# Seven half products for the second matmul in two of every three token groups in place of every second one, and for 17 tokens as well as 16

## The chip, the core and the metric

The kernel runs on one core of a Trainium2 chip. The metric is the device time of one execution in microseconds; unless said otherwise, a number is the median of the fast runs of a kernel. Ratios are the mean time of one kernel's fast runs over that of the kernel before in the same rounds, so not quite the ratio of the medians that stand beside them. Where a length comes from a trace, it is one profiled execution.

In the profiles here TensorE (PE) does the matmuls, VectorE (DVE) elementwise work, transposes and statistics, ScalarE (ACT) activations and copies, GpSimd (POOL) next to nothing (11.1 us, 1% of the span).

## The reference

```python
# x (8, 4224, 192) fp32; weight (8 heads, 7 taps)
out = causal_conv_7_taps(x, softmax(weight))      # one tap set per head of 24 channels
mu, var = mean(out), var(out)                     # over the 192 channels
xn = (out - mu) / sqrt(var + 1e-6) * g_ln
return out + relu(xn @ w_ch1) @ w_ch2             # 192 -> 768 -> 192
```

## The kernel before

Each of 128 partitions holds 33 tokens of each of 8 batches, which the kernel works through in 18 groups: 6, 8, 9 and 10 tokens, then 16 (even groups) and 17 (odd groups) by turns. For group `g` TensorE runs `up(g)` (first matmul, `ph` in the profile; ScalarE applies the ReLU) and then the second matmul, in one of two ways: in full (`down`, `po`) or in seven half products after Strassen and Winograd (`down_fast`, `pd`). Meanwhile VectorE prepares the next group: six of the seven taps (`conv`; the first is ScalarE's), then a transpose (`yt`) which `up(g + 1)` reads. That transpose is called the hand-over below. A group with the seven products is "fast", the others "slow"; F16 is a fast group of 16 tokens, S17 a slow one of 17.

```python
for g in range(NG):
    if g + 2 < NG: load_x(g + 2)
    up(g)
    ...
    if g in FAST:                       # fast group: all of this is VectorE's but down_fast
        conv(g + 1, 1, 4)               # three taps of the next group
        sums_early(g, (0,))             # sums of halves of the hidden layer
        conv(g + 1, 4, 5)
        sums_early(g, (1, 2))
        parts = down_fast(g)            # TensorE: seven products; VectorE: conv(g+1,5,6),
                                        #   sums_late (six ops), the first of three adds
        conv(g + 1, 6, 7)
        transpose(g + 1)                # the hand-over
        stats(g)
        finish_fast(g, *parts)          # two adds, six transposes, residual, store
        continue
    if g + 1 < NG:                      # slow group
        conv(g + 1); transpose(g + 1)
    ...
    stats(g); down(g); finish(g)
```

In `down_fast` the third product reads what `sums_early` wrote, the fifth and the seventh what `sums_late` wrote. VectorE runs its instructions in this order, as its timelines show (in group 9 after the change the taps at 509.72 us start only after the sums that waited for the ReLU until 507.19), and the buffers of the hidden layer, of the transposed input and of the products' results are single.

Of the kernel before, what the change touches and what calls it, by code (L numbers as in the profile page):

```python
# [16 lines left out]
def kernel(  # L17
# [54 lines left out]
    assert max(n for _, _, n in groups) <= J  # L72
    NG = len(groups)

    FAST = set(range(6, NG - 1, 2))
    NFAST = max(groups[g][2] for g in FAST)
    T = C // 2
    CH = NC // 2
# [223 lines left out]
    def conv(g, k0=1, k1=K):  # L302
        n = groups[g][2]
        t = xg[g]
        for k in range(k0, k1):
            for h in range(H):
                cs = slice(h * GRP, h * GRP + GRP)
                nc.vector.scalar_tensor_tensor(  # L308
                    out=y[g][:, 0:n, cs], in0=t[:, k : k + n, cs], scalar=taps[:, h, k : k + 1],
                    in1=y[g][:, 0:n, cs], op0=ALU.mult, op1=ALU.add,  # L310
                )
# [59 lines left out]
    def up(g):  # L371
        n = groups[g][2]
        t = yt[g]
        room = hpool.tile([P, NF * NQ * J * C], F32, tag="ht", name=f"ht{g}")
        if g in FAST:

# [5 lines left out]
        for f in range(NF):  # L382
            fs = slice(f * P, f * P + P)
            for js in blocks(n):
# [12 lines left out]
                for q in range(NQ):  # L397
                    src = ph[q][:, 0:w]
                    if g in FAST:
                        dst = ht[g][:, :, f // FC, f % FC, q, js, :].rearrange("p h j t -> p j h t")  # L400
# [33 lines left out]
    def w2_sums():  # L434
        (b11, b12), (b21, b22) = (
            (w2[:, e * FC : e * FC + FC, 0 : D // 2], w2[:, e * FC : e * FC + FC, D // 2 : D])
            for e in range(2)
        )

        for dst, a, b in ((0, b12, b11), (1, b22, 0), (2, b22, b12), (3, b21, 1)):  # L440
            a, b = (w2sums[:, v] if isinstance(v, int) else v for v in (a, b))
            nc.vector.tensor_tensor(w2sums[:, dst], a, b, op=ALU.subtract)
# [147 lines left out]
    for g in range(NG):  # L590
# [3 lines left out]
        if g == 4:  # L594
            w2_sums()
        if g in FAST:
            conv(g + 1, 1, 4)
# [57 lines left out]
```

## Time and profile before

1045.72 us (1045.59 to 1046.34, 4 runs), granted TensorE clock 1.00. From the chain of waits and VectorE's timeline that the prediction shows:

| part | F16 | S17 | S16 |
|---|---|---|---|
| group, us of TensorE | 58.44 | 66.35 | 62.15 |
| the hand-over is ready, us before TensorE needs it | 2.6 | some 22 | some 25 |

The first row is the sum of two pieces of the chain. The last row is the end of the `yt` transpose against the start of the next group, for S17 and S16 worked out from the timeline.

### The profile page before, as it was taken

The numbers are of one execution on the slowest core, as the hardware profiler recorded it, in microseconds if no ns is written. First come the engines' busy times: TensorE is split into PE (matmuls) and PEld (weight loads), VectorE is DVE, ScalarE is ACT, GpSimd is POOL, SyncE is SP. The second block draws the span as 40 slices with busy tenths as digits, with TensorE's granted clock in tenths as the row PEclk, the third lists the DMA queues.
The fourth block names the chain that finished last, engine by engine and source line by source line (L and its number), as shares of the span: only waits on it lengthen the run. The fifth ranks groups of instructions, "written<-read, shape, count | busy, mean of one in ns | idle before, by whom it ended". The sixth has DMA issues, their size and how long they took to land.

```text
span 1044.5 us, 35348 instructions
## 1 busy us (share of the span) xinstructions
PE 1025.0 (98%) x16088; PEld 661.1 (63%) x16088; DVE 877.0 (84%) x1981; ACT 347.0 (33%) x890; POOL 11.1 (1%) x23
## 2 busy tenths in 40 slices
PE   4999999999999999999999999999999999999998
PEld 2988554358545775458654686556854578545876
DVE  7999999949479996799967999679977899679913
ACT  4442332315034340344304442144412445033320
POOL 1000000000000000000000000000000000000000
PEclk9999999999999999999999999999999999999999
DMA  5113113012030030302112030300303003010101
GB/s 190 60 63 137 47 78 122 1 62 89 3 148 2 13 138 3 148 2 95 57 58 92 3 150 2 140 10 3 150 2 149 1 3 150 2 65 2 54 11 67
DMA packets 7315, 67.15 MB, mean 64 GB/s; under 512 B 1151, under 2 KB 1919, under 8 KB 3326
## 3 DMA queue, kind: packets, MB, share of 16 engines
q1 hardware_dynamic: 6862, 64.91, 16.3%
q8 instruction: 125, 2.05, 0.8%
q14 instruction: 24, 0.20, 0.1%
q10 hardware_dynamic: 304, 0.00, 0.0%
HBM read 38.95 MB, written 25.95 MB: 62 GB/s over the span
## 4 chain that ended last, share of the span: by engine, by line
PE 91%; DVE 7%; DMA 1%; ACT 0%; issue 0%; DVEq 0%; SPq 0%
PE ph L393 47%; PE po L425 29%; PE pd L487 16%; DVE y L308 4%; DMA room<-in_moe_w_ch_dram 1%; DVE yt L320 0%; DVE st L333 0%; DVE y L568 0%; DVE ot L561 0%; ACT room L186 0%; DVE room L194 0%; DVE spare L194 0%; DVE w L200 0%; ACT spare L186 0%; DVE d L355 0%
## 5 line engine op out<-in xcount | busy, mean ns | idle before, releaser
L393 PE MATMUL ph<-yt,w 32*128 32x256 f32 (+4 forms) x7200 | 517.8, 443 | 0.5 <-DVE ot L561 0.5
L393 PEld LDWEIGHTS ph<-yt,w 32*128 32x128 f32 x7200 | 367.9, 185 | 147.9 <-issue 115.5
L308 DVE SCALAR_TENSOR_TENSOR y<-xg,taps,y 128x384 f32<-128x384 f32 (+5 forms) x864 | 431.4, 576 | 0.0
L405 ACT ACTIVATE ht<-ph 128x288 f32<-128x288 f32 (+4 forms) x600 | 222.7, 458 | 545.3 <-PE ph L393 545.2
L425 PE MATMUL po<-ht,w 128*32 128x256 f32 (+6 forms) x5760 | 328.9, 390 | 0.0
L425 PEld LDWEIGHTS po<-ht,w 128*32 128x32 f32 x5760 | 184.6, 110 | 142.7 <-issue 24.8
L561 DVE STREAM_TRANSPOSE ot<-po 128x288 f32<-128x288 f32 (+6 forms) x114 | 47.3, 448 | 105.2 <-PE po L425 105.0
L487 PE MATMUL pd<-ht,w 128*32 128x256 f32 x1296 | 72.3, 379 | 0.0
L487 PE MATMUL pd<-ht,w2sums 128*32 128x256 f32 x1296 | 71.0, 379 | 0.0
L333 DVE BATCH_NORM_STATS2 st<-y 128x6 f32<-128x192 f32 x264 | 69.7, 342 | 0.0
L298 ACT ACTIVATE y<-xg,taps 128x384 f32<-128x384 f32 (+4 forms) x136 | 69.5, 602 | 0.0
L487 PEld LDWEIGHTS pd<-ht,w 128*32 128x32 f32 x1296 | 41.5, 110 | 31.3 <-issue 4.5
L487 PEld LDWEIGHTS pd<-ht,w2sums 128*32 128x32 f32 x1296 | 42.1, 110 | 27.8
L320 DVE STREAM_TRANSPOSE yt<-y 128x3072 f32<-128x3072 f32 (+5 forms) x18 | 56.0, 3112 | 3.0 <-PE ph L393 1.8
L568 DVE SCALAR_TENSOR_TENSOR y<-ot,r,y 128x192 f32<-128x192 f32 x168 | 57.1, 412 | 0.7
L454 DVE TENSOR_TENSOR s<-ht 128x1024 f32<-128x1024 f32 x18 | 22.0, 1222 | 38.7 <-ACT ht L405 38.7
L492 ACT COPY cs<-pd 128x256 f32<-128x256 f32 x72 | 27.0, 375 | 48.8 <-PE pd L487 48.8
L492 ACT COPY part<-pd 128x256 f32<-128x256 f32 x54 | 20.1, 372 | 40.6 <-PE pd L487 40.6
L536 DVE SCALAR_TENSOR_TENSOR y<-ot,r,y 128x192 f32<-128x192 f32 x96 | 32.1, 411 | 0.2
L487 PE MATMUL pd<-s,w2sums 128*32 128x256 f32 x432 | 24.4, 379 | 0.0
L455 DVE TENSOR_TENSOR ht<-ht 128x1024 f32<-128x1024 f32 x18 | 22.1, 1225 | 0.6
L531 DVE STREAM_TRANSPOSE ot<-cs 128x512 f32<-128x512 f32 x36 | 22.0, 674 | 0.0
(70 smaller groups left out, 199.7 us busy)
## 6 DMA issues: line engine op xcount, KB each, us to landing
xg<-in_x_dram SPq DMA_DIRECT2D x7, 2208.0 KB, 12.1
xg<-in_x_dram SPq DMA_DIRECT2D x7, 2112.0 KB, 11.6
out_dram<-y SPq DMA_DIRECT2D x7, 1536.0 KB, 6.0
out_dram<-y SPq DMA_DIRECT2D x6, 1632.0 KB, 6.2
xg<-in_x_dram SPq DMA_DIRECT2D x1, 1536.0 KB, 6.3
xg<-in_x_dram SPq DMA_DIRECT2D x1, 1440.0 KB, 6.0
xg<-in_x_dram SPq DMA_DIRECT2D x1, 1344.0 KB, 10.8
raw<-in_moe_w_ch_dram SPq DMA_DIRECT2D x1, 1152.0 KB, 8.1
```

What stands on the lines that cost most here:

```text
L298: nc.scalar.mul(dst, src, tap)
L308: nc.vector.scalar_tensor_tensor(out=y[g][:, 0:n, cs], in0=t[:, k : k + n, cs], scalar=taps[:, h, k : k + 1], in1=y[g][:, 0:n, cs], op0=AL ...
L320: nc.vector.transpose(yt[g][:, 0:n].rearrange("p j c t -> p (j c t)"), y[g][:, 0:n].rearrange("p j d -> p (j d)"),)
L333: nc.vector.bn_stats(out=st[:, j, :], in_=y[g][:, j, :])
L393: nc.tensor.matmul(ph[q][:, 0:w], w1[rows, c, fs], t[rows, js, c, :], start=(c == 0), stop=(c == NC - 1),)
L405: nc.scalar.activation(dst, src, AF.Relu)
L425: nc.tensor.matmul(bank[C * q : C * q + C, 0:w], w2[:, f, C * c : C * c + C], t[:, f, q, js, :], start=(f == 0), stop=(f == NF - 1),)
L487: nc.tensor.matmul(dst[C * q : C * q + C, 0:w], right[:, f, C * c : C * c + C], left[:, f, q], start=(first and f == 0), stop=(f == FC - 1 ...
L492: nc.scalar.copy(to[:, c], dst[:, 0:w].rearrange("p (j t) -> p j t", t=T))
L536: nc.vector.scalar_tensor_tensor(out=yg[:, j, :], in0=ot[:, j, :], scalar=rstd[g][:, j : j + 1], in1=yg[:, j, :], op0=ALU.mult, op1=ALU.add,)
L561: nc.vector.transpose(ot[:, js, C * c : C * c + C], src.rearrange("p (j t) -> p j t", t=C))
L568: nc.vector.scalar_tensor_tensor(out=yg[:, j, :], in0=ot[:, j, :], scalar=rstd[g][:, j : j + 1], in1=yg[:, j, :], op0=ALU.mult, op1=ALU.add,)
```

## The change

The seven products cost TensorE less than the full one, and the change uses them in eight groups instead of six; the groups of 17 tokens are new to them.

```diff
-    FAST = set(range(6, NG - 1, 2))
+    FAST = {g for g in range(6, NG - 1) if g % 3 != 2}
```

Before: 6, 8, 10, 12, 14, 16. After: 6, 7, 9, 10, 12, 13, 15, 16. For the first time two fast groups follow each other, in the order F16, F17 (6-7, 12-13) and in the order F17, F16 (9-10, 15-16). In the instruction order nothing else moves. The buffers of the products' results become 17 tokens wide, so the adds of a group of 16 have one dimension more; they still take 0.95 us.

## The prediction

One label in the text below is wrong: the worked example, which begins at 415.13 us, is group 8, not group 6 (group 6 begins at 290.33 and has the same lengths), and the slow group after it is 9. The steps use only its lengths.

The forecast's sum is 1045.76 - 9.1 + 1.4 = 1038.1; the lags behind its 1.4 us use the early and late sums of 17 tokens on VectorE, 7.6 and 7.2 us, which took an allowance for each instruction. The measured 7.2 and 6.8 us of 16 tokens times 17/16 give 7.65 and 7.2 (an estimate), so VectorE's 63.7 us and the lags stand on that. In the trace before, one such sum of 1024 elements took 1216 to 1225 ns on average. The 0.1 us for the signal to TensorE, part of the 1.4, was the author's estimate; the only number near it in the trace before is the 0.07 us from TensorE's end to VectorE's start in group 4.

> **What bounds the kernel now.** I read the page's engine shares first, then the chain of waits in order of time, then a table of windows by group, then VectorE's timeline inside one of the groups that use seven half products. Group 6 is the example; the kernel has 18 groups (0 to 17) of 6, 8, 9, 10 and then 16 and 17 tokens by turns, and "fast" below means a group that uses the seven products, "slow" one that doesn't. F16 is a fast group of 16 tokens, S17 a slow one of 17.
>
> ```profile
> span 1044.5 us, 35348 instructions
> ...
> PE 1025.0 (98%) x16088; PEld 661.1 (63%) x16088; DVE 877.0 (84%) x1981; ACT 347.0 (33%) x890; POOL 11.1 (1%) x23
> ...
> PEclk9999999999999999999999999999999999999999
> ```
>
> ```profile
> 381.99 33.14 PE po L425 x576
> 415.13 31.11 PE ph L393 x288
> 446.24 27.33 PE pd L487 x504
> 473.57 33.21 PE ph L393 x576
> 506.79 33.14 PE po L425 x576
> 539.92 31.11 PE ph L393 x288
> ```
>
> In the chain of waits (start, length, what) every piece from 87.07 us to 1039.54 us is TensorE, each beginning where the one before ended. So there TensorE never waits, and each group has a fixed price: F16 = 31.11 + 27.33 = 58.44 us, S17 = 33.21 + 33.14 = 66.35 us. Group 4, the only S16, has pieces of 31.11 (from 161.83) and 31.04 us (from 192.95) in the same view: 62.15 us. ph is the first matmul, po the second in full, pd the second in seven half products.
>
> ```profile
> core 0: us, PE busy (x) PEld busy (x) DVE busy (x) ACT busy (x) POOL busy (x), PEclk, DMA share, GB/s
> ...
> 415.13:473.57 58.44, 58.44 (x796) 30.95 (x796) 51.82 (x86) 23.42 (x52) 1.05 (x1) 1.00 0.18 68
> 473.57:539.92 66.35, 66.35 (x1157) 48.05 (x1156) 57.15 (x147) 19.72 (x57) 0.00 (x0) 1.00 0.16 60
> ```
>
> VectorE is busy 51.8 of 58.4 us and 57.2 of 66.4 us: it looks loose, but its work for group 6 is not done inside group 6's window, as its timeline shows (start, length, line, what, idle before it):
>
> ```profile
> 419.21 13.38 DVE L308 SCALAR_TENSOR_TENSOR y<-xg,taps,y 128x408 f32<-128x408 f32 x24
> 438.06 1.23 DVE L454 TENSOR_TENSOR s<-ht 128x1024 f32<-128x1024 f32 x1 [5.46 <-ACT ht L405]
> ...
> 440.46 4.51 DVE L308 SCALAR_TENSOR_TENSOR y<-xg,taps,y 128x408 f32<-128x408 f32 x8
> ...
> 455.19 3.48 DVE L465 TENSOR_TENSOR ht<-s,ht 128x1024 f32<-128x1024 f32 x3
> 458.60 3.48 DVE L467 TENSOR_TENSOR ht<-ht 128x1024 f32<-128x1024 f32 x3
> ...
> 467.42 3.58 DVE L320 STREAM_TRANSPOSE yt<-y 128x3264 f32<-128x3264 f32 x1
> 470.93 4.21 DVE L333 BATCH_NORM_STATS2 st<-y 128x6 f32<-128x192 f32 x16
> ...
> 488.91 25.48 DVE L308 SCALAR_TENSOR_TENSOR y<-xg,taps,y 128x384 f32<-128x384 f32 x48
> 514.50 3.38 DVE L320 STREAM_TRANSPOSE yt<-y 128x3072 f32<-128x3072 f32 x1
> ```
>
> Group 6 begins on TensorE at 415.13. VectorE joins it at +4.1 us (419.21), idles 5.5 us for the ReLU of the fourth block, hands over the transposed input of group 7 at 470.93 (+55.8; TensorE needs it at +58.44), and is done with group 6 at 488.91 (+73.8), which is 15.3 us into group 7. The slow group gives this lag back.
>
> [...]Here 144 products of 512 columns took 31.04 us, 215.6 ns each[...], 252 of 256 columns 27.33 us, 108.5 ns[...], and 288 of 288 and 256 columns by turns 33.14 us, 115.1 ns[...], and the granted clock is 1.00.[...]
>
> **The change part by part.** Fast groups were 6, 8, 10, 12, 14, 16 (all of 16 tokens). They become 6, 7, 9, 10, 12, 13, 15, 16: four of 16 and four of 17 tokens, so 132 tokens in place of 96. Slow are 8, 11, 14 and 17.
>
> TensorE. A conversion of 17 tokens replaces 33.14 us by 252 products of 272 columns. 272 is the mean of the 288 and 256 that now take 115.07 ns, so 252 x 115.07 = 29.0 us: 4.14 us saved. A conversion of 16 saves 31.04 - 27.33 = 3.71. Before 6 x 3.71 = 22.26; after 4 x 3.71 + 4 x 4.14 = 31.40. Gain 9.1 us, if TensorE still never waits.
>
> VectorE. Its work in a fast group, measured start to start in the timeline above, with next group of 17: six taps 26.7 us, early sums 7.2, late sums 6.8, one add 0.9, transpose 3.5, statistics 7.3, two adds 1.7, output transposes 3.7, residual 5.3: 63 us, against 58.4 of TensorE. F17 with next 16: taps 25.7, early sums 7.6[...], late sums 7.2, adds 2.8, transpose 3.3, statistics 7.6, output 3.9 + 5.6: 63.7 us, against 33.21 + 29.0 = 62.2. Slow groups need some 46 us against 62 to 66. Over a cycle of three (63 + 63.7 + 46 = 173 against 183 to 187 of TensorE) VectorE still fits. But two fast groups in a row are new: the lag of the first is now carried into a second which also wants more than it gives. So I followed it through, times from each group's start on TensorE.
>
> Order F16, F17 (6-7 and 12-13). The second starts with VectorE at +15.3. Three taps to 28.1; early sum 30.7, tap 34.9, two early sums 40.0 (their ReLUs are there by about 34.4); tap 44.3; late sums 51.5; add 52.4; tap 56.8; transpose 60.1. TensorE needs it at 62.2: 2.1 us to spare. TensorE's third product, which reads the early sums, starts at 33.2 + 2 x 4.14 = 41.5; the fifth, which reads the late ones, at 49.8 while the first late sums are ready at 47.9. Nothing waits. VectorE leaves at +79.0, 16.8 into the slow group.
>
> Slow group 8 (S16). Taps and transpose end at 47.0, statistics at 54.3, then VectorE is ahead of the products again: it waits for the last of six. In group 4 the last output transpose began 0.07 us after TensorE's end (224.05) and the residual ended at 230.08, so VectorE enters group 9 at +6.1.
>
> Order F17, F16 (9-10 and 15-16). F17 from +6.1: taps to 18.9, wait for the ReLU to about 23.5, transpose ends at 57.1 (needed 62.2), VectorE leaves at 76.0, i.e. +13.8. F16 from +13.8 with 17-wide taps: 27.2; early sum 29.6, tap 34.0, early sums 38.8 (the third product starts at 38.9); tap 43.3; late sums 46.7 and 50.1 (the fifth product starts at 46.7, and reads the last third of them 0.9 us later); add 51.0; tap 55.5; transpose 59.0, but TensorE needs it at 58.44. Here TensorE waits, 0.6 us plus some 0.1 for the signal. Twice: 1.4 us. Group 11 then starts with VectorE at +17.9; its ninth output bank (of eight) needs the first one transposed at 55.3, and VectorE gets there at 54.4. It just fits.
>
> ScalarE does 21 copies of 272 elements (some 0.39 us, estimated between the 0.375 of 256 and more) and eight first taps in the seven products, as in every fast group now; at 33% busy it is not asked for more than it has. The loads move later, because one load waits for the residual of two groups earlier: issued at +15 to +18, 12 us to landing, needed on ScalarE from about +34. Hidden.
>
> Sum: 1045.76 - 9.1 + 1.4 = 1038.1.
>
> **Rivals.** (1) VectorE becomes the bound. Busy share 84% and 63 us against 58.4 speak for it; the slow third group with 16 to 20 us of spare time speaks against it, as long as the lag is given back there. If each fast group cost 2 us more on VectorE than I reckon (strided 17-token tiles, an add with one more dimension), the order F17, F16 would wait some 4.5 us and F16, F17 some 2, each twice: 13 us, and the time would be 1045.76 - 9.1 + 13 = 1050. (2) No wait at all: my chain is conservative by 1 us a group, and the gain is 9.1: 1036.6. The before timeline fits my durations to 0.1 us, so a whole microsecond is unlikely. (3) A buffer holds: y with three buffers, or the x loads with two, now released by the second fast group's residual, arriving late for ScalarE's first tap. That would show as ScalarE waiting for a transfer[...]. The 4 us between landing (about +30) and need (+34) in the slow group, where ScalarE has nothing else to do, speak against it.
>
> **Range and chances.** Prediction 1038.1 us, 0.7% less. The floor is 1036.6, since nothing else is removed; above it the waits could be several times my 1.4 us. 8 times in 10 within 1036.4 to 1043. 2% is 21 us: the whole saving of TensorE is 9 us, so faster by over 2% is next to impossible, 0.01. Slower by over 2% would need 30 us of new waits, about 7 in each of four pairs, 0.02. Within 2%: 0.97.
>
> **What would show it.** The pd pieces of groups 7, 9, 13, 15 last 29.0 us and po pieces of S16 31.04. The idle time of TensorE or its weight load before ph, put down to VectorE's transpose, appears only at the starts of groups 11 and 17, under 1 us each. VectorE's first tap after group 7's residual starts some 16.8 us into group 8, that of group 11's some 17.9 us into it. VectorE's idle time before the early sums vanishes in groups 7, 10, 13, 16. I'd be wrong if pd or po waits for VectorE in the middle of a group, if waits also stand at the starts of groups 8 and 14, or if 272 columns cost more than 115 ns.

## The result, and the profile after

1038.12 us (1038.00 to 1038.75, 4 runs) against 1045.72: ratio 0.9927, 95% interval 0.9910 to 0.9945. The page after:

```profile
span 1036.2 us, 33980 instructions
...
PE 1015.6 (98%) x15368; PEld 644.4 (62%) x15368; DVE 910.0 (88%) x1987; ACT 363.9 (35%) x932; POOL 11.1 (1%) x23
...
PE 74%; DVE 22%; issue 2%; DMA 1%; ACT 1%; DVEq 0%; SPq 0%
```

TensorE lost 9.4 us of busy time and VectorE gained 33, and the chain that ended last, 91% TensorE before, now goes through VectorE for 22% of the span. That share does not mean that VectorE cost 22%: the chain is followed back from one wait to its releaser, and a short wait is enough to switch it to VectorE's long unbroken row of work. How long the waits are is told by TensorE's own timeline (start, length, what, and in brackets the idle time before it):

```profile
410.49 31.18 PE L393 MATMUL ph<-yt,w 32*128 32x512 f32 x288
...
472.64 33.28 PE L393 MATMUL ph<-yt,w 32*128 32x288 f32 x576
...
534.87 31.18 PE L393 MATMUL ph<-yt,w 32*128 32x512 f32 x288
...
589.32 4.07 PE L487 MATMUL pd<-ht,w 128*32 128x256 f32 x72
594.06 33.28 PE L393 MATMUL ph<-yt,w 32*128 32x288 f32 x576 [0.68 <-DVE yt L320]
...
964.65 33.28 PE L393 MATMUL ph<-yt,w 32*128 32x288 f32 x576 [0.68 <-DVE yt L320]
```

These are the starts of groups 8, 9, 10, 11 and 17. Only 11 and 17, the groups after F17, F16, have an idle time, and it is put down to the hand-over. The windows by group give the price of each (busy times and counts as in the prediction's table of windows):

```profile
core 0: us, PE busy (x) PEld busy (x) DVE busy (x) ACT busy (x) POOL busy (x), PEclk, DMA share, GB/s
...
348.27:410.49 62.22, 62.22 (x1084) 45.70 (x1080) 61.50 (x118) 27.25 (x77) 0.00 (x0) 1.00 0.17 64
534.87:594.06 59.19, 58.51 (x796) 30.86 (x793) 58.54 (x100) 24.20 (x54) 1.05 (x1) 1.00 0.17 67
```

Group 7 (F17) takes 62.22 us where it took 66.35 as S17. Group 10 takes 59.19 us where F16 without a wait takes 58.44. VectorE's lag shows in its own timeline:

```profile
427.24 26.69 DVE L308 SCALAR_TENSOR_TENSOR y<-xg,taps,y 128x408 f32<-128x408 f32 x48
...
478.80 12.79 DVE L308 SCALAR_TENSOR_TENSOR y<-xg,taps,y 128x384 f32<-128x384 f32 x24
...
548.67 13.39 DVE L308 SCALAR_TENSOR_TENSOR y<-xg,taps,y 128x408 f32<-128x408 f32 x24
561.98 1.23 DVE L454 TENSOR_TENSOR s<-ht 128x1024 f32<-128x1024 f32 x1
...
590.34 3.58 DVE L320 STREAM_TRANSPOSE yt<-y 128x3264 f32<-128x3264 f32 x1
593.84 4.22 DVE L333 BATCH_NORM_STATS2 st<-y 128x6 f32<-128x192 f32 x16
```

Subtract each group's start on TensorE: VectorE enters slow group 8 at 427.24 - 410.49 = +16.8 us, group 9 at 478.80 - 472.64 = +6.2 (the slow group gave 10.6 us back), group 10 at +13.8. There it no longer idles before the early sums, which had 5.5 us of idle time before them in the kernel before, and is through with the hand-over at +59.0, when TensorE would have started at +58.44.

What sets the +13.8 is not the lag at which VectorE enters group 9. There VectorE waits twice for the ReLU, 6.2 us in all:

```profile
496.19 1.29 DVE L454 TENSOR_TENSOR s<-ht 128x1088 f32<-128x1088 f32 x1 [4.59 <-ACT ht L405]
...
507.19 1.29 DVE L454 TENSOR_TENSOR s<-ht 128x1088 f32<-128x1088 f32 x1 [1.62 <-ACT ht L405]
```

After the second wait (+34.6 in group 9) it has no idle time up to the hand-over in group 10. So an earlier entry into group 9, or one up to some 6 us later, would have changed nothing behind it (an estimate from these two waits): the slow group 8 had given back more than was needed, and the late hand-over is made of VectorE's work since that ReLU.

### The profile page after: what moved, and what is told of

Same layout as the page of the kernel before. It is cut to its first block, busy times and chain, and to the rows that moved or that the text cites. A ratio compares the mean times of both kernels' runs of the same rounds, so it can differ in the third digit from the quotient of the medians.

```text
span 1036.2 us, 33980 instructions
## 1 busy us (share of the span) xinstructions
PE 1015.6 (98%) x15368; PEld 644.4 (62%) x15368; DVE 910.0 (88%) x1987; ACT 363.9 (35%) x932; POOL 11.1 (1%) x23
## 4 chain that ended last, share of the span: by engine, by line
PE 74%; DVE 22%; issue 2%; DMA 1%; ACT 1%; DVEq 0%; SPq 0%
PE ph L393 41%; PE po L425 22%; DVE y L308 11%; PE pd L487 11%; DVE yt L320 2%; DVE st L333 1%; DVE y L536 1%; DVE ht L467 1%; DVE ht L455 1%; DVE s L454 1%; DVE ot L531 1%; DMA room<-in_moe_w_ch_dram 1%; DVE ht L465 1%; DVE cs L517 0%; DVE y L568 0%
## 5 line engine op out<-in xcount | busy, mean ns | idle before, releaser
L425 PE MATMUL po<-ht,w 128*32 128x288 f32 (+6 forms) x4032 | 258.0, 417 | 0.0
L425 PEld LDWEIGHTS po<-ht,w 128*32 128x32 f32 x4032 | 128.6, 110 | 128.2 <-issue 65.7
L487 PE MATMUL pd<-ht,w 128*32 128x256 f32 (+1 forms) x1728 | 99.2, 386 | 0.0
L487 PE MATMUL pd<-ht,w2sums 128*32 128x256 f32 (+1 forms) x1728 | 97.6, 386 | 0.0
L492 ACT COPY cs<-pd 128x256 f32<-128x256 f32 (+1 forms) x96 | 36.6, 381 | 70.1 <-PE pd L487 70.1
L454 DVE TENSOR_TENSOR s<-ht 128x1024 f32<-128x1024 f32 (+1 forms) x24 | 30.1, 1254 | 25.3 <-ACT ht L405 25.3
L492 ACT COPY part<-pd 128x256 f32<-128x256 f32 (+1 forms) x72 | 27.3, 380 | 55.3 <-PE pd L487 55.3
L487 PE MATMUL pd<-s,w2sums 128*32 128x256 f32 (+1 forms) x576 | 33.5, 386 | 0.0
L455 DVE TENSOR_TENSOR ht<-ht 128x1024 f32<-128x1024 f32 (+1 forms) x24 | 30.2, 1259 | 1.1
L531 DVE STREAM_TRANSPOSE ot<-cs 128x512 f32<-128x512 f32 (+1 forms) x48 | 30.1, 691 | 0.0
```

Source lines behind the costliest of these rows:

```text
L425: nc.tensor.matmul(bank[C * q : C * q + C, 0:w], w2[:, f, C * c : C * c + C], t[:, f, q, js, :], start=(f == 0), stop=(f == NF - 1),)
L455: nc.vector.tensor_tensor(a[:, 1, 0, f], a[:, 0, 0, f], a[:, 1, 0, f], op=ALU.subtract)
L487: nc.tensor.matmul(dst[C * q : C * q + C, 0:w], right[:, f, C * c : C * c + C], left[:, f, q], start=(first and f == 0), stop=(f == FC - 1 ...
L492: nc.scalar.copy(to[:, c], dst[:, 0:w].rearrange("p (j t) -> p j t", t=T))
```

## The experiments

Theory: TensorE's work sets the time, 9.1 us less with these eight fast groups than with the six; the one new wait is the late hand-over after F17, F16, because VectorE carries the lag of the first fast group into the second; a slow group pays the lag back. Rivals: the waits have another cause (a buffer or a load), or VectorE is the bound throughout, or TensorE's work alone counts.

| run | median us | before, same rounds | ratio, 95% interval |
|---|---|---|---|
| first add after the hand-over | 1037.12 | 1045.51 | 0.9918 (0.9903 to 0.9932) |
| hand-over cut in two | 1037.58 | 1045.95 | 0.9919 (0.9904 to 0.9933) |
| six fast groups, all of 17 tokens | 1044.11 | 1045.51 | 0.9984 (0.9968 to 1.0001) |
| groups 6 to 16 all fast | 1053.41 | 1045.51 | 1.0076 (1.0061 to 1.0091) |
| one extra add | 1044.41 | 1045.51 | 0.9989 (0.9974 to 1.0004) |
| a third of an extra add | 1040.56 | 1045.52 | 0.9952 (0.9937 to 0.9967) |
| kernel before, three extra adds | 1049.43 | 1045.52 | 1.0037 (1.0022 to 1.0052) |
| adds on GpSimd | 1055.02 | 1045.52 | 1.0080 (1.0055 to 1.0105) |
| adds on GpSimd, groups 5 to 16 all fast | 1063.71 | 1045.52 | 1.0170 (1.0153 to 1.0187) |
| late add, nine fast groups | 1034.18 | 1045.95 | 0.9888 (0.9871 to 0.9904) |

All ten gave the right result.

**The wait removed in two ways.** First, one add that nothing needs before the hand-over is done after it:

```diff
         sums_late(g, 0); sums_late(g, 1)          # in down_fast, cut
-        nc.vector.tensor_tensor(c11, c11, part[:, 0], op=ALU.add)
 ...
+        c11 = cs[:, 0:CH, :, 0]                    # in finish_fast, after the hand-over
+        nc.vector.tensor_tensor(c11, c11, part[:, 0], op=ALU.add)
```

> The changed kernel, with the first of the three adds on VectorE moved from before the next group's transpose to after it; same work, same result. Theory (TensorE waits only at the starts of groups 11 and 17, 0.68 us each, because VectorE delivers the transposed input late): the add is 0.87 to 0.92 us before the transpose, so both waits vanish; 1038.1 - 1.4 = about 1036.8 us, and no idle time of TensorE before ph is left to VectorE. Rival (a late load, a buffer of y or of PSUM holds the start of these groups): unchanged, 1038.1 us, and the waits stay.

Measured 1037.12 us, and no idle time of TensorE before `ph` is left from group 6 on: group 10 takes 58.44 us (535.54 to 593.98), and group 11 begins without a wait.

```profile
593.98 33.28 PE L393 MATMUL ph<-yt,w 32*128 32x288 f32 x576
```

Second, the hand-over itself is cut, so that TensorE can begin on the first 9 tokens:

```diff
-        nc.vector.transpose(yt[g][:, 0:n]..., y[g][:, 0:n]...)
+        for js in blocks(n):
+            nc.vector.transpose(yt[g][:, js]..., y[g][:, js]...)
```

> The changed kernel with the transpose of a group of 17 tokens cut in two, 9 tokens and then 8, as TensorE reads them; same result. Theory (in groups 10 and 16 TensorE waits for this one instruction and for nothing else): the first part is there some 1.6 us before the whole was, the wait was 0.68 us, so both waits vanish at the cost of 0.1 us of VectorE; 1036.8 us. Rival (some other hand-over, such as a bank of PSUM or the ReLU's buffer, ends at about the same time and would take its place): the time stays near 1038.1 and the idle time before ph in groups 11 and 17 is put down to something else.

Measured 1037.58 us, and again no wait before `ph` in groups 11 and 17, nor one in its place. The two ways touch different things and remove the same wait; no buffer or load was behind it. In time this is worth 0.1%, the width of the intervals, so the verdict is from the traces: the waits are gone. The medians agree within 0.8 us of 1036.8.

**The price of a conversion of 17 tokens by itself.** As many fast groups as before, by turns as before, but the odd ones.

```diff
-    FAST = {g for g in range(6, NG - 1) if g % 3 != 2}
+    FAST = set(range(5, NG - 1, 2))
```

> Groups 5, 7, 9, 11, 13, 15 fast: six as before and alternating as before, but all of 17 tokens. Theory (a conversion of 17 tokens is worth 4.14 us against 3.71, and alternation gives the lag back): no wait on TensorE, 6 x 0.43 = 2.6 us less than before, 1043.1 us. Rival (272 columns in a half product cost more than the mean of 288 and 256, or 17 tokens cost VectorE more): at or above 1045.7 us.

Measured 1044.11 us, 1 us above. In the trace the prices are as expected: group 7 takes 62.22 us (348.90 to 411.12), S16 groups 62.15, TensorE waits nowhere after group 5. From the start of group 4 to the end this run's trace takes 879.9 us against 882.7 in the kernel before: 2.8 us less, where 2.6 were expected. Ahead of the changed part it is 0.6 us later (`ph` of group 4 starts at 162.37 us here, at 161.76 in the kernel before and at 161.30 in the changed kernel; this start-up differs from trace to trace by up to 1.2 us). The rest of what is missing is within the spread of the runs: the kernel before took 1045.20 to 1046.45 us in these rounds. So the 4.14 us stand by the traces; the time over all shows only part of them, and its interval reaches 1.

**No slow group between.**

```diff
-    FAST = {g for g in range(6, NG - 1) if g % 3 != 2}
+    FAST = set(range(6, NG - 1))
```

> All groups 6 to 16 use the seven half products, no slow group between them. Theory (VectorE needs 63 to 64 us per fast group, against 58.4 and 62.2 on TensorE, and only slow groups pay the lag back): after the first two groups VectorE sets the pace, about 63.4 us a group, no better than a slow group of 16; slower than before, about 1053 us, with TensorE idle 3 to 6 us in each group of 16 in part in the middle of the group. Rival (time follows TensorE's work, waits are incidental): 11 conversions save 6 x 3.71 + 5 x 4.14 = 43 us against 22.3 of before, 1025 us.

Measured 1053.41 us: three more groups get the cheaper product than in the changed kernel, and the kernel is slower than before by 0.8%. TensorE's timeline in group 10 of this run:

```profile
575.29 0.61 PE L487 MATMUL pd<-ht,w2sums 128*32 128x256 f32 x8
577.82 0.64 PE L487 MATMUL pd<-ht,w2sums 128*32 128x256 f32 x8 [1.92 <-DVE ht L455]
580.21 12.69 PE L487 MATMUL pd<-ht,w2sums 128*32 128x256 f32 x200 [1.75 <-DVE ht L455]
```

The third product waits for the early sums (L455), twice: the lag is now so large that VectorE is late in the middle of the group already. Groups 10 and 11 together take 536.38 to 663.06 = 126.7 us, which is VectorE's 63 + 63.7 of the prediction, not TensorE's 120.7. The granted clock fell after these two waits (0.50 from 581 to 583 us in the windows), but that is not what sets the pace: VectorE has no idle time in its timeline from 530 to 800 us. Here VectorE is the bound.

**Doses of extra work.** An add into a buffer that nobody reads any more, ahead of the hand-over; whole, or a third of the width.

```diff
         nc.vector.tensor_tensor(c11, c11, part[:, 0], op=ALU.add)
+        nc.vector.tensor_tensor(part[:, 0], c11, part[:, 0], op=ALU.add)
```

> The changed kernel with one more add of the same kind (some 0.95 us with its wait) on VectorE before each fast group's hand-over, into a buffer that nobody reads any more; result unchanged. Theory: the pairs of 17 then 16 tokens carry 0.95 us of lag from the first group into the second and add 0.95 there, so each of the two waits grows by about 1.9 us; the pairs of 16 then 17 stay just inside their slack of 2.1 us. About 1038.1 + 3.8 = 1041.9 us. Rival (waits incidental): 1038.1 us, or 8 x 0.95 = 7.6 more, 1045.7, if VectorE is the bound throughout.

> As the run with one extra add, but the extra add covers a third of the width (some 0.43 us). Theory: each of the two waits grows by 2 x 0.43 to some 1.5 us, 1038.1 + 1.7 = 1039.8 us, and no other group waits. The run with one whole add showed that an idle time of 2.4 us of TensorE brings its clock to one half for some 3 us afterwards, 1.5 us more. If the clock falls already after 1.5 us, the two groups cost that again: 1042.8 us; if not, the granted clock stays at 1.00.

The 0.43 us of the third was the author's estimate. A straight line through the 0.95 us of 768 elements and the 1.22 us of 1024 in the trace before gives 0.41 us for 256 (an estimate as well).

The waits before `ph` grew from 0.68 to 1.60 us (a third) and 2.40 us (one), and stayed at the starts of groups 11 and 17; the first line is of the run with a third, the second of that with one add:

```profile
595.21 33.28 PE L393 MATMUL ph<-yt,w 32*128 32x288 f32 x576 [1.60 <-DVE yt L320]
596.20 34.79 PE L393 MATMUL ph<-yt,w 32*128 32x288 f32 x576 [2.40 <-DVE yt L320]
```

With one add a part of the price has moved into the middle of groups 10 and 16: there weight loads wait up to 0.5 us for an early and 0.3 us for a late sum. Group 10 as a whole takes 61.21 us in place of 59.19 (60.12 with a third). So 0.95 us of work on VectorE costs TensorE 2.0 us in each pair, as expected: once in the first group and once in the second. But the time with one add is 1044.41, 2.5 us above the expectation. The windows in group 10's end and group 11's beginning of that run show why:

```profile
592.00:596.20 4.20, 1.80 (x36) 0.83 (x28) 4.17 (x3) 0.74 (x2) 0.00 (x0) 0.96 0.00 0
596.20:597.00 0.80, 0.80 (x8) 0.70 (x12) 0.80 (x5) 0.00 (x0) 0.00 (x0) 0.50 0.00 0
...
599.00:600.00 1.00, 1.00 (x17) 0.81 (x17) 1.00 (x5) 0.00 (x0) 0.00 (x0) 0.84 0.00 0
600.00:601.00 1.00, 1.00 (x24) 0.90 (x20) 0.90 (x6) 0.04 (x1) 0.00 (x0) 1.00 0.00 0
```

The column after POOL is the granted clock. After 2.4 us of idle time it is one half for some 3.1 us of TensorE's work, and `ph` of group 11 takes 34.79 us in place of 33.28: 1.5 us on top of the wait. In group 17 `ph` takes 34.97, 1.7 us more. 2 x 2.0 + 1.5 + 1.7 = 7.2, of the 7.4 us by which this trace's span exceeds that of the changed kernel. This profiled run is also the slowest of its four (1045.43 us; clock 0.996). The others took 1043.95 to 1044.56 us at a clock of 0.998, as if it had fallen once and not twice; they left no trace, so that is not shown. With a third of an add (1.60 us of idle time) the clock stayed at 1.00 and `ph` took 33.28; 1040.56 us against the expected 1039.8.

**When the clock falls.** From the views of the traces that the experiments left: waits of TensorE, the granted clock that the windows show for the work after them, and how long that work took beside the same work without a wait.

| run, work that waited (start, us) | idle before it, us | clock after it | length, us (without a wait) |
|---|---|---|---|
| changed kernel, `ph` of group 11 (594.06) | 0.68 | 1.00 | 33.28 (33.28) |
| all fast, `ph` of group 9 (473.78) | 1.42 | 1.00 | 33.28 (33.28) |
| a third, `ph` of group 11 (595.21) | 1.60 | 1.00 | 33.28 (33.28) |
| all fast, third product of group 8 (453.52) | 1.75 | 1.00 | 11.07 |
| one add, `ph` of group 11 (596.20) | 2.40 | 0.50 | 34.79 (33.28) |
| one add, `ph` of group 17 (970.39) | 2.41 | 0.50 | 34.97 (33.28) |
| adds on GpSimd, `ph` of group 8 (413.72) | 2.68 | no window | 31.18 (31.18) |
| adds on GpSimd, `ph` of group 14 (791.56) | 2.68 | no window | 32.88 (31.18) |
| adds on GpSimd, `ph` of group 11 (600.10) | 3.49 | 0.54 to 0.57 | 34.97 (33.28) |
| all fast, third product of group 10 (580.21) | 1.92, then 1.75 | 0.50 | 12.69 (11.07 in group 8) |

So no single wait of up to 1.75 us lowered the clock or lengthened the work behind it. Of the table's five single waits from 2.40 us on, four lengthened that work by 1.5 to 1.7 us, and one of the two equal waits of 2.68 us did not. Two waits of 1.92 and 1.75 us with 0.64 us of work between them lowered the clock where one of 1.75 us had not. What decides it was not shown: no experiment varied the length or the place of a wait by itself.

**The same dose where it has room.** Three such adds in the kernel before.

> The kernel before (fast groups alternate) with three extra adds of some 0.93 us on VectorE ahead of the hand-over in each of the six fast groups, result unchanged. Theory (a lone fast group has 2.5 us of slack at the hand-over and the slow one after it gives the lag back): 2.8 us of extra work costs some 0.3 us in each of six groups, 1.9 us in all, 1047.5 us. Rival (extra work on VectorE is paid in full in each group wherever it stands): 6 x 2.8 = 17 us, 1062 us.

Measured 1049.43 us, 3.9 us above the kernel before. Each fast group takes 59.07 us (289.95 to 349.02) in place of 58.44. VectorE was slowed by some 3.0 us in each and TensorE by 0.63, so the slack absorbed most of it and the rival's 17 us are out. The expectation of 0.3 us per group took 2.8 us for the three adds and 0.1 for the signal from VectorE to TensorE; the trace has 2.98 and 0.2.

**The adds on another engine.** GpSimd is idle, so its 1% share invites this:

```diff
-        nc.vector.tensor_tensor(c11, c11, part[:, 0], op=ALU.add)
+        nc.gpsimd.tensor_tensor(c11, c11, part[:, 0], op=ALU.add)
 ...                                                # the adds into c21 and c22 likewise
```

> The changed kernel with the three adds of each fast group on GpSimd in place of VectorE (2.6 to 2.8 us of VectorE's time per fast group). Theory: the hand-over in the pairs of 17 then 16 tokens comes some 3.5 us earlier (0.9 of its own, 2.7 of the group before), the two waits vanish, 1036.7 us; no more is to be had, since TensorE's work is the rest. It falls short if GpSimd's adds slow VectorE's own instructions or come too late for the output transposes.

> All groups 5 to 16 use the seven half products, with the three adds on GpSimd. Theory (capacity of VectorE is what stopped the version with all groups fast at 1053 us): VectorE now needs some 60.3 us for a fast group of 16 and 60.9 for one of 17, against 58.4 and 62.2 of TensorE, so it just keeps up on average; 12 conversions save 6 x 3.71 + 6 x 4.14 = 47.1 us against 22.3 of before, some 4 us of waits in the groups of 16: 1025 us. Rival (two fast groups in a row fail for another reason than VectorE's work, for instance a single buffer of the second product's results): stays near 1049 us, as with all groups 6 to 16.

Both expectations failed: 1055.02 and 1063.71 us, slower than the kernel before. VectorE was relieved of 2.7 us in each fast group and lost more. In the first of the two runs, group 6, VectorE's taps and GpSimd's add:

```profile
337.25 7.72 DVE L308 SCALAR_TENSOR_TENSOR y<-xg,taps,y 128x408 f32<-128x408 f32 x8
```

```profile
329.91 9.11 POOL L517 TENSOR_TENSOR cs<-cs,part 128x768 f32<-128x768 f32 x1 [22.16 <-ACT part L492]
```

Eight taps that take 4.5 us alone take 7.7 beside GpSimd's adds, and the add that took VectorE 0.95 us takes GpSimd 1.85 to 9.1 (spans on GpSimd are rough). The single instructions tell how: six of the eight taps keep their 0.63 us, and two take 2.2, each until 0.44 us after the end of an add; in group 7 three more are held, until 0.42 us after it. So here single taps were held until an add was over; it is not that all of them ran slower. The late sums beside the first add kept their 3.48 us for three, and that add took 9.1. Below, the second of the two taps is one that was held:

```profile
341.05 2.80 DVE L308 SCALAR_TENSOR_TENSOR y<-xg,taps,y 128x408 f32<-128x408 f32 x2
341.56 1.85 POOL L528 TENSOR_TENSOR cs<-cs,part 128x768 f32<-128x768 f32 x1 [2.54 <-ACT cs L492]
```

The hand-over comes later, not earlier: TensorE waits 2.7 to 3.5 us at the starts of groups 8, 11, 14 and 17, and the clock falls after three of them (`ph` of group 8, after 2.68 us, took 31.18 us; that of group 14, after the same wait, 32.88). One of the four runs of the first version took 1049.63 us at a clock of 0.996, the others 1054.5 us and more at 0.993 or 0.994. So these runs say nothing for or against the capacity of VectorE; they tell that the adds moved to GpSimd did not leave VectorE alone. (The 1049 us in the rival of the second expectation is a slip: the run with groups 6 to 16 all fast took 1053.41.)

**A version that beats both.** With the add after the hand-over there is room for a ninth fast group.

```diff
-    FAST = {g for g in range(6, NG - 1) if g % 3 != 2}
+    FAST = {5, 6, 8, 9, 11, 12, 13, 15, 16}        # and the late add
```

> The first add after the hand-over, as in the run with the late add, and nine fast groups in place of eight: 5, 6, 8, 9, 11, 12, 13, 15, 16 (four of 16 tokens, five of 17). Theory: by the same account of lags, TensorE saves 4 x 3.71 + 5 x 4.14 = 35.5 us against 22.3 of before, and waits 0.4 us for a bank of PSUM in group 7 and 0.9 us for an early sum in group 13, the third fast group in a row; 1045.5 - 13.2 + 1.3 = 1033.6 us. If the account of lags is off by a microsecond in the row of three, the clock may fall after a longer wait and cost 1.5 us more: 1036 us.

Measured 1034.18 us. TensorE's one wait is the one expected, in group 13, the third fast group in a row:

```profile
757.73 11.67 PE L487 MATMUL pd<-ht,w2sums 128*32 128x272 f32 x200 [0.66 <-DVE ht L455]
```

The wait for a bank in group 7 is there too, on the weight load (0.6 us for VectorE's output transpose): group 7 takes 344.33 to 411.00 = 66.67 us, 0.32 more than S17 without it. The clock stayed at 1.00.

## Why the prediction was right

The range held, and the point was off by less than 0.1 us, partly by luck: start-up alone moves a trace by more. By its own steps:

- *TensorE never waits before, so its price per group is the time.* Right; unchanged pieces kept their lengths. The 108.5 ns of a product is a mean, not the time that one takes: in the trace four matmuls of 256 columns start within 20 ns of each other, the next four 216 ns later, and each product has two records (504 for 252).
- *4.14 us per conversion of 17 tokens, 272 columns at 115.07 ns.* Right: the second matmul of group 7 lasts 410.49 - 381.48 = 29.01 us against 29.0, and the group is 4.13 us shorter. The run with odd groups alone shows it without pairs.
- *VectorE's order, and the sums of 17 tokens.* The trace after shows them: in group 9 the taps at 509.72 came only after the sums that had waited for the ReLU, and 1088 elements took 1283 to 1292 ns on average, 1024 elements 1218 to 1225.
- *F16, F17 has 2.1 us to spare.* Right: the hand-over of group 7 ended at +60.0 (60.1 predicted), no wait in groups 8 and 14. The dose of 0.95 us, twice, left them without a wait, as it had to.
- *The slow group pays the lag back.* Right: +16.8 into group 8, +6.2 into group 9 (16.8 and 6.1 predicted). The run without slow groups shows the other side.
- *F17, F16 waits 0.6 us plus the signal, twice.* Right: +13.8 into group 10 as predicted, ready at +59.0, group 10 longer by 0.75 us (0.7 predicted). The signal is some 0.2 us, not 0.1, read as the start of VectorE's next instruction (593.84) to that of the matmul (594.06), or 0.14 us from the end that the profile records (590.34 + 3.58). Both ways of removing the wait show its cause.
- *Group 11's ninth bank just fits, VectorE at +54.4.* Right: 648.32 - 594.06 = +54.3, and TensorE did not wait.
- *ScalarE's copies of 272 elements 0.39 us, loads hidden.* Right: 0.386 us. The loads' later issue is seen (group 10's load at 427.78, landed 12.7 us later, at +30.0 of group 8; ScalarE's first tap follows at +33.1).
- *Rival 1, 2 us more per fast group, would give 1050.* Not needed here, but the sum left out the clock: it treated a wait as costing its own length. In the runs that held for single waits of up to 1.75 us, and for four of five from 2.40 us on it did not.

The profile's spans differ by 8.3 us, the medians by 7.6. Some 0.5 us of the first lies before group 4, in the start-up, and isn't the change's.

## What to carry to other kernels

Where two engines run in step, follow the lag of the second from group to group instead of comparing busy shares: what counts is when each hand-over is ready, and a group that runs the second engine over its time is fine as long as another gives the time back before the lag meets a deadline. The first lever is then the order of work ahead of the hand-over; one add moved behind it let a ninth group take the cheaper product. A wait's own length is not always its price: here single waits of up to 1.75 us cost just that, and four of five from 2.40 to 3.49 us cost 1.5 to 1.7 us more; the windows of three of the four show the clock at 0.50 to 0.57. And before moving work to an idle engine, measure what it does to the busy one beside it.
